# An mLSTM layer with two feed-forward blocks: the 64-by-64 products of each attention tile in one group, a 128-row spreading product, fixed PSUM banks, and a last store over three queues

## The chip, the cores and the metric

The kernel runs on one core of a Trainium2 chip, in one launch. The metric is the device time of one execution in microseconds (us), lower is better. TensorE (PE) multiplies, VectorE (DVE), ScalarE (ACT) and GpSimd (POOL) work on elements, SyncE (SP) issues most transfers.

## What is computed

An mLSTM recurrence over 768 positions, for 2 batches of 8 heads of width 40, whose output (1536 tokens of 320) passes two feed-forward blocks of inner width 2048:

```python
for t in range(S):
    m_new = np.maximum(f_gate[:, :, t] + m, i_gate[:, :, t])
    f_stab = np.exp(f_gate[:, :, t] + m - m_new)
    i_stab = np.exp(i_gate[:, :, t] - m_new)
    m = m_new
    C = f_stab * C + i_stab * outer(v_t, k_t)
    n = f_stab * n + i_stab * k_t
    y[:, :, t] = sigmoid(o_gate_t) * (C @ q_t) / np.maximum(abs(n @ q_t), 1.0)
x = hinge2(x @ w_in) @ w_out
x = softplus(x @ w_in2) @ w_out2
```

## The kernel before

**Attention.** The recurrence is done by chunks: 12 tiles of 64 positions, both batches side by side on the 128 partitions (64 each). For tile n, TensorE makes: `bc` (L422), one product that spreads the forget gates of all heads over the partitions, with 64 rows of weights (`sel`); `qkp` (L452), keys times queries, 16 products of 64 by 64; `pv` (L474), the masked weights times the values, and `pv` again (L482), the state times the decayed queries, 16 products each; `stp` (L521), the state's update, 16 products; and `tr` (L540), three 128-by-128 transposes of the result `y` into `xh`, the feed-forward input. Between them DVE makes the decay mask `f` by a scan over `bc` (L436) and multiplies it by `qkp` (L463), prepares `qd` (L467), the denominators `den` (L495, L496), `y` (L505), and adds `stp` to `state` (L534), which POOL has decayed before (L525). POOL also makes `vi`, `ve`, `m` and the gated `sig`. The small products use one half of the array's rows (64 or 40) and half of its columns; the profile counts each as two records, so 16 are shown as x32.

**Feed-forward.** Tokens go in three blocks of 512. A step is one slice of 128 of the inner width: `h`, 8 products of 128x512 (L620, `up`), an activation on ACT and DVE, a split of the result into a high part `gh` and a low part `gl` (L669, L673), and the products of `down1` (8 of 128x512, L687 to L693) or `down2` (12 of 128x320, L750 to L752), which accumulate over 16 steps. There are 48 steps in each of the two feed-forward blocks. Each weight slice is loaded once (`raw`, L565, 704 KB), unpacked from 64-bit floats by two ACT operations and one DVE operation (`v`, L571 to L582), and split into high and low parts `w` (L593 on ACT, L600 on DVE or POOL). Two `raw` and two `v` buffers exist. The slices of the first feed-forward block are needed in the first 16 steps, which is also where tiles 4 to 7 run.

**The order.** A planner (class `Plan`) takes every operation with an estimated cost and, for some PE operations, a place `at`, works out due times, and emits each engine's instructions in the order of a list schedule; the order is fixed when the program is built. Feed-forward step g has place 10·g. The list `where` gives each tile its places: tiles 0 to 3 (`n < EARLY`) come before the first step, in what is called the head below; of tiles 4 to 11 each four run within 16 steps. While PE has nothing else at the start, the planner inserts `fill` products (L387), which change no result.

**PSUM.** Eight banks: `h` has two, `d0`, `d1`, `d2` one each, and the pool `a` three, which `bc`, `qkp`, `pv`, `stp` and `tr` take in rotation.

**The end.** The last block's four output tiles `o` are copied from PSUM (L765 on DVE, L767 on ACT) and each is stored by two transfers (L782), one from SP's queue and one from ACT's.

Of the kernel before, what the change touches and what calls it, by code (L numbers as in the profile page):

```python
# [30 lines left out]
WARM = 200  # L31
EARLY = 4


class Plan:
# [15 lines left out]

    def add(self, eng, cost, emit, reads=(), writes=(), new=(), at=None, after=0.0, port=False, duty=1.0, fill=False):
        self.tasks.append(dict(
            eng=eng, cost=cost, emit=emit, reads=list(reads), writes=list(writes),
            new=list(new), at=at, after=after, port=port, duty=duty, fill=fill, i=len(self.tasks)))

# [14 lines left out]
    def run(self, start):  # L71
# [57 lines left out]
        for i in range(n):  # L129
            if not left[i]:  # L130
                enter(i)
        port, filling = 0.0, True
# [46 lines left out]
def mlstm_moe_moe(ctx: ExitStack, tc: tile.TileContext, gates, qk, tok, ident, w1, w2, out):  # L179
    nc = tc.nc  # L180

    def pool(name, bufs, stack=ctx, **kw):
        return stack.enter_context(tc.tile_pool(name=name, bufs=bufs, **kw))

    BUFS = dict(raw=2, v=2, w=NF, u=3, gh=4, gl=3, xr=1, qk=2, tok=2, m=1, f=2, dec=2, qd=2, sig=2, vi=2, ve=2,
                den=2, y=2, v2=10, e=3, o=4, h=2, d0=1, d1=1, d2=1, a=3)
    pools, tiles = {}, {}
# [3 lines left out]
    for name in ("raw", "v", "w", "u", "gh", "gl", "xr"):  # L191
        pools[name] = pool(name, BUFS[name])
    for name in ("h", "d0", "d1", "d2", "a"):
        pools[name] = pool("ps_" + name, BUFS[name], space=PSUM)
# [97 lines left out]
    for s, (c0, c1) in enumerate(SEG):  # L292
# [68 lines left out]
        def t(s=s, c0=c0, c1=c1):  # L361
            ps = new("a", ("isp", s), [128, 4, 16])
            for k in range((c1 - c0) // 2):
                nc.tensor.transpose(ps[:, k, :], tiles["gi",][:, (c0 + 2 * k) * C:(c0 + 2 * k + 2) * C], id_sb[0:16, 0:16])
        add("pe", 0.02 * (c1 - c0), t, duty=0.5, reads=[(gi, s), (("id",),)], writes=[(("isp", s),)],
            new=[("a", ("isp", s))], at=-100 + s)

# [23 lines left out]
    def attention(c, at):  # L391
# [17 lines left out]

        qtag, btag = ("d0", "h") if n < EARLY else ("a", "a")  # L410

        def t(e):
            eng = nc.gpsimd if e == "pool" else nc.vector
            eng.tensor_tensor(
                out=new("m", ("m", n), [64, H, C], F32R), in0=gr[:, None, c * C:(c + 1) * C].to_broadcast([64, H, C]),
                in1=own[:, :, None].to_broadcast([64, H, C]), op=ALU.mult)
# [36 lines left out]
        add("pe", 1.1, t, duty=0.75, reads=[(QK,)], writes=[(("qkp", n),)], new=[(qtag, ("qkp", n))], at=at[0])  # L453

# [22 lines left out]
        add("pe", 1.1, t, duty=0.75, reads=[(FK,), (VI,)], writes=[(("pv", n),)], new=[("a", ("pv", n))], at=at[1])  # L477
        if c > 0:
            def t():
                for h in range(H):  # L480
                    for p, k in zip(half, keys):
                        nc.tensor.matmul(  # L482
                            tiles["pv", n][p, h, :], tiles[QD][k, h, :], state[k, h, :], start=False, stop=(h == H - 1))
            add("pe", 1.0, t, duty=0.75, reads=[(QD,), (ST,)], writes=[(("pv", n),)], at=at[1] + 0.5)

# [4 lines left out]
        def t():  # L490
            nc.scalar.activation(out=new("den", DN, [128, H, 1]), in_=tiles["pv", n][:, :, D:V1], func=ACTF.Abs)
        add("act", 0.16, t, reads=[*ATT, (("pv", n),)], writes=[(DN,)], new=[("den", DN)])

# [20 lines left out]
        if c < NC - 1:  # L514
            def t():
                ps = new("a", ("stp", n), [128, H, V1])
# [5 lines left out]
            add("pe", 1.1 if n < EARLY else 0.75, t, duty=0.75, reads=[(TK,), (VE,)], writes=[(("stp", n),)], new=[("a", ("stp", n))], at=at[1] + 1)  # L522
            if c > 0:
# [13 lines left out]
        def t():  # L537
            ps = new("a", ("tr", n), [128, 3, L])
            for i in range(3):
                nc.tensor.transpose(ps[:, i, :], tiles[Y][:, i * 128:(i + 1) * 128], id_sb)  # L540
        add("pe", 0.34, t, reads=[(Y, 0), (Y, 1)], writes=[(("tr", n),)], new=[("a", ("tr", n))], at=at[2])
        j, o = block_of(n * L)
# [17 lines left out]
    def weights(l, f):  # L560
# [11 lines left out]
        add("act", act(WC), t, reads=[(R,)] + ([*ATT] if l else []), writes=[(V,)], new=[(tag, V)])  # L572
# [5 lines left out]
        add("act", act(WC), t, writes=[(V,)])  # L578

# [8 lines left out]
    def weights_split(l, f, V):  # L588
        W = ("w", l, f)

        def t():
            w = new("w", W, [128, 2 * WC], F32R)
            nc.scalar.copy(w[:, 0:WC], tiles[V].bitcast(F32))  # L593
        add("act", act(WC), t, reads=[(V,)], writes=[(W, 0)], new=[("w", W)])

# [137 lines left out]
    def down2(j, f, at):  # L733
# [21 lines left out]
        if e:  # L755
            for i in range(m):
# [13 lines left out]

                if j == len(BLOCKS) - 1 and i == m - 1:
                    copies([("act", 0, DM // 2), ("dve", DM // 2, DM)])
                else:
                    copies([("dve" if i % 2 else "act", 0, DM)])

                for b in range(B):
                    q = "act" if j == len(BLOCKS) - 1 and b else "sp"

                    def t(b=b, i=i, O=O, q=q):
                        r0 = b * S + (t0 // L + i) * C  # L780
                        eng = nc.scalar if q == "act" else nc.sync
                        eng.dma_start(out=out[r0:r0 + C, :], in_=tiles[O][64 * b:64 * b + 64, :])  # L782
                    add(q, 0.6, t, reads=[(O, 0), (O, DM // 2)], after=2.0)
# [106 lines left out]
```

## Time and profile before

| | |
|---|---|
| three timed runs | 437.7, 437.94, 439.21 us (median 437.94) |
| the profiled execution, its own time | 440.93 us |
| its span in the trace | 439.1 us |
| PE busy | 427.7 us (97% of the span) |
| DVE, ACT, POOL busy | 296.2, 272.7, 52.9 us |
| granted TensorE clock, mean | 0.993 of full speed |
| read from HBM, written | 38.57 MB, 2.02 MB |

The time around the span is 440.93 − 439.1 = 1.83 us. Busy time of PE is modelled: matmuls are pipelined, so that a 128x512 product of 0.39 us is followed by the next one after 0.23 us. What PE spends is therefore read from one start to the next.

### The profile page before, as it was taken

The numbers are of one execution on the slowest core, as the hardware profiler recorded it, in microseconds if no ns is written. First come the engines' busy times: TensorE is split into PE (matmuls) and PEld (weight loads), VectorE is DVE, ScalarE is ACT, GpSimd is POOL, SyncE is SP. The second block draws the span as 40 slices with busy tenths as digits, with TensorE's granted clock in tenths as the row PEclk, the third lists the DMA queues.
The fourth block names the chain that finished last, engine by engine and source line by source line (L and its number), as shares of the span: only waits on it lengthen the run. The fifth ranks groups of instructions, "written<-read, shape, count | busy, mean of one in ns | idle before, by whom it ended". The sixth has DMA issues, their size and how long they took to land.

```text
span 439.1 us, 8150 instructions
## 1 busy us (share of the span) xinstructions
PE 427.7 (97%) x3315; PEld 354.9 (81%) x3315; DVE 296.2 (67%) x467; ACT 272.7 (62%) x474; POOL 52.9 (12%) x64
## 2 busy tenths in 40 slices
PE   8989999998999999999999999999999999999994
PEld 3766887877787878787888888899999999999994
DVE  6989999978548454556877779555565555655552
ACT  4645988786426445478999987555555555555551
POOL 3743241312122211000000000000000000000000
PEclk9999999998999999999999999999999999999998
DMA  6889657657031200034354500000020000010002
GB/s 231 260 300 301 214 183 234 214 194 233 18 120 37 84 1 1 1 117 156 110 187 157 170 29 0 0 2 0 1 52 9 1 1 0 24 37 2 0 1 60
DMA packets 12214, 41.11 MB, mean 94 GB/s; under 512 B 1905, under 2 KB 3569, under 8 KB 12177
## 3 DMA queue, kind: packets, MB, share of 16 engines
q1 hardware_dynamic: 11856, 40.27, 28.1%
q8 instruction: 26, 0.43, 0.4%
q10 hardware_dynamic: 320, 0.33, 0.3%
q14 instruction: 12, 0.09, 0.1%
HBM read 38.57 MB, written 2.02 MB: 92 GB/s over the span
## 4 chain that ended last, share of the span: by engine, by line
PE 87%; DMA 4%; DVE 3%; ACT 3%; issue 2%; POOL 0%; SPq 0%; DVEq 0%; POOLq 0%; ACTq 0%
PE h L620 39%; PE d L692 5%; PE d L691 5%; PE d L693 4%; PE d L751 3%; PE a L751 3%; PE a L752 3%; PE d L752 3%; PE d L750 3%; PE a L750 3%; PE d L687 3%; PE pv L474 2%; PE d L688 2%; PE pv L482 2%; DMA qk<-in_qk_dram 2%
## 5 line engine op out<-in xcount | busy, mean ns | idle before, releaser
L620 PE MATMUL h<-xh,w 128*128 128x512 f32 x576 | 180.3, 395 | 1.1 <-ACT xh L545 0.6
L620 PEld LDWEIGHTS h<-xh,w 128*128 128x128 f32 x576 | 108.0, 188 | 25.2 <-DVE u L637 1.1
L673 DVE TENSOR_TENSOR gl<-u,gh 128x512 fp32r<-128x512 f32 x96 | 69.0, 720 | 41.7 <-ACT gh L669 36.5
L669 ACT CAST gh<-u 128x512 fp32r<-128x512 f32 x96 | 59.5, 620 | 52.2 <-DVE u L660 32.9
L620 PE MATMUL h<-xl,w 128*128 128x512 f32 x192 | 75.7, 394 | 0.1
L660 DVE TENSOR_TENSOR u<-u,e 128x512 f32<-128x512 f32 x48 | 33.2, 692 | 31.8 <-ACT e L656 31.8
L656 ACT ACTIVATE e<-e 128x512 f32<-128x512 f32 x48 | 30.4, 633 | 34.6 <-DVE e L651 34.5
L637 DVE SCALAR_TENSOR_TENSOR u<-u,h 128x512 f32<-128x512 f32 x48 | 32.7, 681 | 15.7 <-ACT u L633 15.2
L628 ACT ACTIVATE u<-h 128x512 f32<-128x512 f32 x48 | 28.4, 592 | 22.3 <-PE h L620 22.0
L620 PEld LDWEIGHTS h<-xl,w 128*128 128x128 f32 x192 | 36.0, 188 | 6.8 <-DVE xl L550 0.4
L692 PE MATMUL d<-gh,w 128*128 128x512 f32 x96 | 37.9, 394 | 0.0
L691 PE MATMUL d<-gh,w 128*128 128x512 f32 x96 | 37.8, 394 | 0.0
L693 PE MATMUL d<-gl,w 128*128 128x512 f32 x96 | 37.6, 391 | 0.0
L651 DVE SCALAR_TENSOR_TENSOR e<-u,h 128x512 f32<-128x512 f32 x48 | 33.0, 687 | 6.0
L582 DVE SCALAR_TENSOR_TENSOR v<-raw,v 128x704 int32<-128x704 int32 x32 | 29.5, 925 | 9.7 <-ACT v L575 9.7
L647 ACT ACTIVATE u<-h 128x512 f32<-128x512 f32 x48 | 28.7, 599 | 10.2 <-PE h L620 10.2
L600 DVE TENSOR_TENSOR w<-v,w 128x704 fp32r<-128x704 f32 (+2 forms) x46 | 29.7, 673 | 4.2 <-ACT w L593 4.1
L571 ACT ACTIVATE v<-raw 128x704 f32<-128x704 int8 x32 | 27.0, 842 | 8.2 <-DMA raw<-in_w_dram 5.7
L633 ACT ACTIVATE u<-u 128x512 f32<-128x512 f32 x48 | 30.2, 630 | 0.4
L751 PE MATMUL d<-w,gh 128*128 128x320 f32 x96 | 29.6, 309 | 0.0
L752 PE MATMUL a<-w,gl 128*128 128x320 f32 x96 | 29.6, 309 | 0.0
L752 PE MATMUL d<-w,gl 128*128 128x320 f32 x96 | 29.6, 309 | 0.0
(92 smaller groups left out, 672.4 us busy)
## 6 DMA issues: line engine op xcount, KB each, us to landing
raw<-in_w_dram SPq DMA_DIRECT2D x32, 704.0 KB, 4.2
qk<-in_qk_dram SPq DMA_DIRECT2D x12, 512.0 KB, 5.0
tok<-in_tok_dram SPq DMA_DIRECT2D x12, 496.0 KB, 4.8
dec<-scr_d SPq DMA_DIRECT2D x22, 128.0 KB, 4.4
out_dram<-o SPq DMA_DIRECT2D x20, 80.0 KB, 2.1
out_dram<-o ACTq DMA_DIRECT2D x4, 80.0 KB, 2.2
consts<-in_ident_dram SPq DMA_DIRECT2D x1, 132.0 KB, 2.6
gf<-in_gates_dram SPq DMA_DIRECT2D x1, 48.0 KB, 2.0
```

The costliest lines, as they stand in the source:

```text
L620: nc.tensor.matmul(hp, a, x, start=(i == 0), stop=(i == len(ops) - 1))
L637: nc.vector.scalar_tensor_tensor(out=tiles[U], in0=tiles[U], scalar=1.0, in1=tiles[HP], op0=ALU.min, op1=ALU.max)
L651: nc.vector.scalar_tensor_tensor(out=new("e", E, [128, n]), in0=tiles[M], scalar=-2.0, in1=tiles[HP], op0=ALU.mult, op1=ALU.add)
L656: nc.scalar.activation(out=tiles[E], in_=tiles[E], func=ACTF.Softplus)
L660: nc.vector.tensor_tensor(out=tiles[M], in0=tiles[M], in1=tiles[E], op=ALU.add)
L669: nc.scalar.copy(new("gh", GH, [128, n], F32R), tiles[G])
L673: nc.vector.tensor_tensor(out=new("gl", GL, [128, n], F32R), in0=tiles[G], in1=tiles[GH].bitcast(F32), op=ALU.subtract)
L691: nc.tensor.matmul(d[i], hi[:, k], gh, start=s, stop=False)
L692: nc.tensor.matmul(d[i], lo[:, k], gh, start=False, stop=False)
L693: nc.tensor.matmul(d[i], hi[:, k], gl, start=False, stop=e)
L751: nc.tensor.matmul(d, gh[:, k], lo, start=False, stop=False)
L752: nc.tensor.matmul(d, gl[:, k], hi, start=False, stop=e)
```

## The change

1. **Places.** `GROUP` gives each of the tiles 4 to 11 one place, every 34 units from 23 on. `pv`, the state product and `stp` of a tile stand there, and `qkp` of the next tile right behind them (`where[n - 1][2] + 1.5`). `bc` stands 25 units ahead of its group, `tr` 15 behind.
2. **The planner** knows which products are small (`small=True`): once it has emitted a small one it prefers others that are due within 8 units (`STAY`), and it adds 0.1 to a product's cost at a change of kind (`SWITCH`). In the first 60 units DVE, ACT and POOL may wait for a more urgent operation (`PATIENT`). `act(c)` is estimated somewhat higher.
3. **The spreading product** has 128 rows in place of 64: `sel`, `own`, `m` and `gr` are 128 rows high (rows beyond the gates are zero).
4. **PSUM.** The pool `a` becomes three pools of one bank. From tile 4 on `bc` and `stp` use `ax`, `qkp` uses `ay`, `pv` and `tr` use `az`; ahead of that `qkp` alternates between `d0` and `d1`.
5. **Operations.** In the second feed-forward block the cast of `w` may run on DVE too. `den` and the unpacking of the weights depend on the table load, so that it cannot come between them.
6. **The last block's stores** go over SP (four), POOL (two, output tiles 0 and 1) and ACT (two, tiles 2 and 3), and the last tile is copied whole by DVE.

```diff
+GROUP = [23 + 34 * i for i in range(8)]
...
+    PATIENT, MARGIN, SHARE, UNTIL = ("dve", "act", "pool"), 3.0, 0.4, 60.0
+    SWITCH, STAY = 0.1, 8.0
...
                 i = min(near, key=lambda i: (due[i], i))
+                if e == "pe" and small:
+                    i = min((k for k in near if ts[k]["small"] and due[k] < due[i] + self.STAY), key=lambda k: due[k], default=i)
+                if e in self.PATIENT and now < self.UNTIL:
+                    urgent = [k for k in q if due[k] < due[i] - self.MARGIN and now < begin[k] < now + ts[i]["cost"] * self.SHARE]
+                    if urgent:
+                        i = min(urgent, key=lambda k: (begin[k], k))
...
-                    t["dur"] = self.clock(now, t["cost"], t["duty"])
+                    t["dur"] = self.clock(now, t["cost"] + (self.SWITCH if t["small"] != small else 0.0), t["duty"])
+                    small = t["small"]
...
-                den=2, y=2, v2=10, e=3, o=4, h=2, d0=1, d1=1, d2=1, a=3)
+                den=2, y=2, v2=10, e=3, o=4, h=2, d0=1, d1=1, d2=1, ax=1, ay=1, az=1)
...
-    id_sb, own, side = consts[:, 0:128], consts[0:64, 128:136], consts[0:64, 136:264]
+    id_sb, own, side = consts[:, 0:128], consts[:, 128:136], consts[:, 136:264]
...
-    sel = const.tile([64, 128], F32R)
-    gr = const.tile([64, S], F32)
+    sel = const.tile([128, 128], F32R)
+    gr = const.tile([128, S], F32)
...
-        qtag, btag = ("d0", "h") if n < EARLY else ("a", "a")
+        qtag, btag, rtag = (f"d{n % 2}", "h", "ay") if n < EARLY else ("ay", "ax", "az")
...
-            new=[(btag, ("bc", n))], at=at[0] - 1)
+            new=[(btag, ("bc", n))], at=at[0])
...
-            ps = new("a", ("pv", n), [128, H, V1])
+            ps = new("az", ("pv", n), [128, H, V1])
...
-        def t():
+        def t(e="act"):
...
+                nc.vector.tensor_copy(w, v)
-        add("act", act(WC), t, reads=[(V,)], writes=[(W, 0)], new=[("w", W)])
+        add("act|dve" if l else "act", act(WC), t, reads=[(V,)], writes=[(W, 0)], new=[("w", W)])
...
-                if j == len(BLOCKS) - 1 and i == m - 1:
-                    copies([("act", 0, DM // 2), ("dve", DM // 2, DM)])
-                else:
-                    copies([("dve" if i % 2 else "act", 0, DM)])
-
+                copies([("dve" if i % 2 else "act", 0, DM)])
                 for b in range(B):
-                    q = "act" if j == len(BLOCKS) - 1 and b else "sp"
+
+                    q = ("sp", "pool", "sp", "pool", "sp", "act", "sp", "act")[B * i + b] if j == len(BLOCKS) - 1 else "sp"
...
-    where, g0 = {}, 0
...
-                where[first + i] = [10 * (g0 + (4 * i + k) * 4 / m) + 3 for k in (0, 1, 3)]
...
+    where = {n: [-61 + 10 * n, -60 + 10 * n, -57 + 10 * n, -54 + 10 * n] for n in range(EARLY)}
+    for n in range(EARLY, NC):
+        p = GROUP[n - EARLY]
+        where[n] = [p - 25, where[n - 1][2] + 1.5, p, p + 15]
```

On PE, around tiles 8 and 9 (the first number in a name is the tile; of `h` and `d` the last is the step), before:

```order
L620 MATMUL h_0_1_0_1662<-xh1_137,w_0_0_550 128x512 x3
L422 MATMUL bc_8_1675<-m_8_1473,sel_132 128x512
L452 MATMUL qkp_8_1679<-qk_8_1239 64x64 x16
L687 MATMUL d2_0_0_916<-gh_0_0_13_1590,w_0_13_1404 128x512
...
L620 MATMUL h_0_1_1_1717<-xh1_137,w_0_1_572 128x512 x3
L474 MATMUL pv_8_1728<-vi_8_1385,f_8_1696 64x41 x16
L482 MATMUL pv_8_1728<-state_135,qd_8_1420 64x41 x16
L521 MATMUL stp_8_1765<-ve_8_1712,tok_8_1348 40x41 x16
L687 MATMUL d2_0_0_916<-gh_0_0_14_1639,w_0_14_1477 128x512
```

and now:

```order
L486 MATMUL pv_8_1689<-vi_8_1428,f_8_1621 64x41 x16
L494 MATMUL pv_8_1689<-state_141,qd_8_1468 64x41 x16
L533 MATMUL stp_8_1726<-ve_8_1631,tok_8_1361 40x41 x16
L464 MATMUL qkp_9_1748<-qk_9_1386 64x64 x16
L635 MATMUL h_0_1_0_1770<-xh1_143,w_0_0_556 128x512
...
L708 MATMUL d1_0_0_917<-gl_0_0_13_1660,w_0_13_1466 128x512
L434 MATMUL bc_9_1802<-m_9_1623,sel_138 128x512
L635 MATMUL h_0_1_1_1805<-xh1_143,w_0_1_659 128x512
```

`bc` and `qkp` stood as a pair of their own one step ahead of the group; now `qkp` of tile 9 closes the group of tile 8, and `bc` of tile 9 stands alone among the 128-row products.

On PE, in the head, from `qkp` of tile 3 to the first `h`, before (the rows left out are 9, 2 and 11 fills):

```order
L452 MATMUL qkp_3_508<-qk_3_432 64x64 x16
L474 MATMUL pv_2_533<-vi_2_408,f_2_382 64x41 x16
L482 MATMUL pv_2_533<-state_135,qd_2_430 64x41 x16
L540 MATMUL tr_1_574<-consts_129,y_1_505 128x128 x3
...
L521 MATMUL stp_3_601<-ve_3_531,tok_3_405 64x41 x16
...
L474 MATMUL pv_3_631<-vi_3_476,f_3_482 64x41 x16
L482 MATMUL pv_3_631<-state_135,qd_3_578 64x41 x16
L540 MATMUL tr_2_676<-consts_129,y_2_623 128x128 x3
...
L452 MATMUL qkp_4_711<-qk_4_464 64x64 x16
L422 MATMUL bc_4_736<-m_4_629,sel_132 128x512
L540 MATMUL tr_3_740<-consts_129,y_3_728 128x128 x3
```

and now (left out are 1, 2, 7 and 7 fills):

```order
L464 MATMUL qkp_3_534<-qk_3_446 64x64 x16
L533 MATMUL stp_2_561<-ve_2_456,tok_2_347 64x41 x16
L552 MATMUL tr_1_581<-consts_135,y_1_482 128x128 x3
...
L486 MATMUL pv_3_594<-vi_3_486,f_3_464 64x41 x16
L494 MATMUL pv_3_594<-state_141,qd_3_579 64x41 x16
L533 MATMUL stp_3_640<-ve_3_515,tok_3_426 64x41 x16
L552 MATMUL tr_2_665<-consts_135,y_2_587 128x128 x3
...
L434 MATMUL bc_4_676<-m_4_638,sel_138 128x512
...
L552 MATMUL tr_3_698<-consts_135,y_3_688 128x128 x3
...
L464 MATMUL qkp_4_719<-qk_4_470 64x64 x16
L533 MATMUL stp_4_742<-ve_4_715,tok_4_585 40x41 x16
```

`pv` of tile 2 now comes ahead of `qkp` of tile 3, `stp` of tile 4 has come in from behind the first two steps, and 17 fills stand where 22 stood.

At the end, on ACT before:

```order
L767 COPY o_2_0_4594<-d2_1_2_0_4152 128x320
L767 COPY o_2_2_4598<-a_1_2_2_4160 128x320
L767 COPY o_2_3_4600<-a_1_2_3_4164 128x160
L782 DMA out_0_dram<-o_2_0_4594 64x320
L782 DMA out_0_dram<-o_2_1_4596 64x320
L782 DMA out_0_dram<-o_2_2_4598 64x320
L782 DMA out_0_dram<-o_2_3_4600 64x320
```

and now, on ACT and then on POOL:

```order
L782 COPY o_2_0_4593<-d2_1_2_0_4151 128x320
L782 COPY o_2_2_4597<-ay_1_2_2_4159 128x320
L794 DMA out_0_dram<-o_2_2_4597 64x320
L794 DMA out_0_dram<-o_2_3_4599 64x320
...
L794 DMA out_0_dram<-o_2_0_4593 64x320
L794 DMA out_0_dram<-o_2_1_4595 64x320
```

ACT issues two transfers in place of four and copies no half tile; POOL issues the other two; SP's four stay.

## Rows read from the trace of the kernel before

**Rows 1.** Busy time by stretch: stretch, its length; PE, PEld, DVE, ACT, POOL busy (instructions); granted clock; DMA share; GB/s.

```profile
50.00:75.00 25.00, 25.00 (x223) 20.11 (x222) 23.87 (x39) 20.80 (x38) 8.35 (x10) 1.00 0.62 207
75.00:100.00 25.00, 24.48 (x243) 19.24 (x242) 21.96 (x37) 19.62 (x36) 5.68 (x6) 1.00 0.58 198
100.00:125.00 25.00, 23.83 (x217) 19.03 (x215) 16.47 (x28) 12.31 (x23) 5.00 (x6) 0.93 0.41 132
```

**Rows 2.** Chain that ended last, two steps of the second feed-forward stretch: start, length, what.

```profile
225.15 1.86 PE h L620 x8
228.85 1.86 PE h L620 x8
```

**Rows 3.** The same chain, 137 to 148 us, around tile 9.

```profile
139.05 0.42 PE bc L422
139.47 1.08 PE qkp L452 x32
140.55 0.43 PE d L687
...
144.46 1.06 PE pv L474 x32
145.52 0.93 PE pv L482 x32
146.46 0.61 PE stp L521 x32
```

**Rows 4.** Instructions of PE in the head, in order of time: start, length, instruction, [idle before].

```profile
27.50 1.15 PE L452 MATMUL qkp<-qk 64*64 64x64 f32 x32 [1.20 <-DMA qk<-in_qk_dram]
28.45 1.11 PE L474 MATMUL pv<-vi,f 64*64 64x41 f32 x32
...
35.40 1.11 PE L482 MATMUL pv<-state,qd 40*64 40x41 f32 x32
...
36.82 2.54 PE L387 MATMUL fill<-warm 128*128 128x512 bf16 x11
...
40.80 0.55 PE L540 MATMUL tr<-consts,y 128*128 128x128 f32 x3
41.91 0.50 PE L620 MATMUL h<-xh,w 128*128 128x512 f32 x1 [0.57 <-ACT xh L545]
```

**Rows 5.** PE at tile 7, in order of time.

```profile
103.55 1.13 PE L474 MATMUL pv<-vi,f 64*64 64x41 f32 x32 [1.17 <-DVE f L463]
```

**Rows 6.** DVE ahead of that, in order of time.

```profile
101.85 0.95 DVE L600 TENSOR_TENSOR w<-v,w 128x64 fp32r<-128x64 f32 x2
102.72 0.68 DVE L463 TENSOR_TENSOR f<-qkp,f 128x512 f32<-128x512 f32 x1
```

**Rows 7.** Busy time by stretch, as in Rows 1: small products in the head, and tile 7.

```profile
14.40:20.20 5.80, 5.66 (x162) 5.08 (x161) 5.70 (x10) 3.18 (x7) 4.43 (x5) 1.00 0.78 222
...
104.40:109.00 4.60, 4.60 (x80) 4.09 (x77) 4.12 (x10) 2.19 (x5) 1.74 (x2) 0.63 0.76 234
```

**Rows 8.** Line L782, the stores: duration ns min/median/max, first and last start us.

```profile
L782 SPq DMA_DIRECT2D out_dram<-o x20: 467/567/603, 323.7 to 434.5; - x20
...
L782 ACTq DMA_DIRECT2D out_dram<-o x4: 557/612/784, 433.9 to 436.0; - x4
...
DMA to landing us min/median/max: 2.0/2.1/2.3
```

**Rows 9.** Copies at the end, in order of time.

```profile
432.62 0.49 DVE L765 COPY o<-a 128x320 f32<-128x320 f32 x1 [2.00 <-PE a L752]
...
433.50 0.33 DVE L765 COPY o<-a 128x160 f32<-128x160 f32 x1 [0.39 <-PE a L752]
```

**Rows 10.** Tile 5: PE, then DVE, in order of time.

```profile
64.10 0.79 PE L521 MATMUL stp<-ve,tok 64*40 64x41 f32 x32
...
68.71 1.00 DVE L534 TENSOR_TENSOR state<-stp,state 40x328 f32<-40x328 f32 x2
```

**Rows 11.** Chain that ended last, the one weight load on it.

```profile
83.06 7.27 DMA raw<-in_w_dram
```

More of the change, by code (lines that the diff above doesn't have):

```diff
@@ L50, in __init__, with add @@
         self.fast, self.busy, self.edge = False, 0.0, self.WINDOW
-    def add(self, eng, cost, emit, reads=(), writes=(), new=(), at=None, after=0.0, port=False, duty=1.0, fill=False):
+    def add(self, eng, cost, emit, reads=(), writes=(), new=(), at=None, after=0.0, port=False, duty=1.0, fill=False, small=False):
         self.tasks.append(dict(
             eng=eng, cost=cost, emit=emit, reads=list(reads), writes=list(writes),
-            new=list(new), at=at, after=after, port=port, duty=duty, fill=fill, i=len(self.tasks)))
+            new=list(new), at=at, after=after, port=port, duty=duty, fill=fill, small=small, i=len(self.tasks)))
     def clock(self, now, cost, duty):
@@ L131, in run @@
                 enter(i)
-        port, filling = 0.0, True
+        port, filling, small = 0.0, True, False
         for _ in range(n):
@@ L192, in mlstm_moe_moe @@
         pools[name] = pool(name, BUFS[name])
-    for name in ("h", "d0", "d1", "d2", "a"):
+    for name in ("h", "d0", "d1", "d2", "ax", "ay", "az"):
         pools[name] = pool("ps_" + name, BUFS[name], space=PSUM)
@@ L361, in t @@
         def t(s=s, c0=c0, c1=c1):
-            ps = new("a", ("isp", s), [128, 4, 16])
+            ps = new("ax", ("isp", s), [128, 4, 16])
             for k in range((c1 - c0) // 2):
@@ L414, in t @@
             eng.tensor_tensor(
-                out=new("m", ("m", n), [64, H, C], F32R), in0=gr[:, None, c * C:(c + 1) * C].to_broadcast([64, H, C]),
-                in1=own[:, :, None].to_broadcast([64, H, C]), op=ALU.mult)
+                out=new("m", ("m", n), [128, H, C], F32R), in0=gr[:, None, c * C:(c + 1) * C].to_broadcast([128, H, C]),
+                in1=own[:, :, None].to_broadcast([128, H, C]), op=ALU.mult)
         add("dve|pool", vec(512), t, port=True, reads=[*ATT, (("gr",), s, 0), (("gr",), s, 1), (("id",),)], writes=[(("m", n),)],
@@ L452, in t @@
                     nc.tensor.matmul(ps[p, h, :], q()[p, 1, h, :], q()[p, 0, h, :], start=True, stop=True)
-        add("pe", 1.1, t, duty=0.75, reads=[(QK,)], writes=[(("qkp", n),)], new=[(qtag, ("qkp", n))], at=at[0])
+        add("pe", 1.1, t, duty=0.75, small=True, reads=[(QK,)], writes=[(("qkp", n),)], new=[(qtag, ("qkp", n))], at=at[1])
         if c < NC - 1:
@@ L476, in t @@
                         start=(h == 0), stop=(c == 0 and h == H - 1))
-        add("pe", 1.1, t, duty=0.75, reads=[(FK,), (VI,)], writes=[(("pv", n),)], new=[("a", ("pv", n))], at=at[1])
+        add("pe", 1.1, t, duty=0.75, small=True, reads=[(FK,), (VI,)], writes=[(("pv", n),)], new=[("az", ("pv", n))], at=at[2])
         if c > 0:
@@ L483, in t @@
                             tiles["pv", n][p, h, :], tiles[QD][k, h, :], state[k, h, :], start=False, stop=(h == H - 1))
-            add("pe", 1.0, t, duty=0.75, reads=[(QD,), (ST,)], writes=[(("pv", n),)], at=at[1] + 0.5)
+            add("pe", 1.0, t, duty=0.75, small=True, reads=[(QD,), (ST,)], writes=[(("pv", n),)], at=at[2] + 0.5)
         def t():
@@ L491, in t @@
             nc.scalar.activation(out=new("den", DN, [128, H, 1]), in_=tiles["pv", n][:, :, D:V1], func=ACTF.Abs)
-        add("act", 0.16, t, reads=[*ATT, (("pv", n),)], writes=[(DN,)], new=[("den", DN)])
+        add("act", 0.16, t, reads=[*ATT, *TAB, (("pv", n),)], writes=[(DN,)], new=[("den", DN)])
         def t():
@@ L515, in t @@
             def t():
-                ps = new("a", ("stp", n), [128, H, V1])
+                ps = new("ax", ("stp", n), [128, H, V1])
                 for h in range(H):
@@ L521, in t @@
                         nc.tensor.matmul(ps[o, h, :], tk()[p, k0:k0 + w], tiles[VE][p, h, :], start=True, stop=True)
-            add("pe", 1.1 if n < EARLY else 0.75, t, duty=0.75, reads=[(TK,), (VE,)], writes=[(("stp", n),)], new=[("a", ("stp", n))], at=at[1] + 1)
+            add("pe", 1.1 if n < EARLY else 0.75, t, duty=0.75, small=True, reads=[(TK,), (VE,)], writes=[(("stp", n),)], new=[("ax", ("stp", n))], at=at[2] + 1)
             if c > 0:
@@ L537, in t @@
         def t():
-            ps = new("a", ("tr", n), [128, 3, L])
+            ps = new(rtag, ("tr", n), [128, 3, L])
             for i in range(3):
                 nc.tensor.transpose(ps[:, i, :], tiles[Y][:, i * 128:(i + 1) * 128], id_sb)
-        add("pe", 0.34, t, reads=[(Y, 0), (Y, 1)], writes=[(("tr", n),)], new=[("a", ("tr", n))], at=at[2])
+        add("pe", 0.34, t, reads=[(Y, 0), (Y, 1)], writes=[(("tr", n),)], new=[(rtag, ("tr", n))], at=at[3])
         j, o = block_of(n * L)
@@ L571, in t @@
             nc.scalar.activation(out=v.bitcast(F32), in_=top, func=ACTF.Prelu, bias=-56.0, alpha=2.0 ** -40)
-        add("act", act(WC), t, reads=[(R,)] + ([*ATT] if l else []), writes=[(V,)], new=[(tag, V)])
+        add("act", act(WC), t, reads=[(R,), *TAB] + ([*ATT] if l else []), writes=[(V,)], new=[(tag, V)])
         def t():
@@ L577, in t @@
                 alpha=2.0 ** 40)
-        add("act", act(WC), t, writes=[(V,)])
+        add("act", act(WC), t, reads=TAB, writes=[(V,)])
         def t():
@@ L589, in weights_split @@
         W = ("w", l, f)
-        def t():
-            w = new("w", W, [128, 2 * WC], F32R)
-            nc.scalar.copy(w[:, 0:WC], tiles[V].bitcast(F32))
-        add("act", act(WC), t, reads=[(V,)], writes=[(W, 0)], new=[("w", W)])
+        def t(e="act"):
+            w, v = new("w", W, [128, 2 * WC], F32R)[:, 0:WC], tiles[V].bitcast(F32)
+            if e == "act":
+                nc.scalar.copy(w, v)
+            else:
+                nc.vector.tensor_copy(w, v)
+        add("act|dve" if l else "act", act(WC), t, reads=[(V,)], writes=[(W, 0)], new=[("w", W)])
         def t(e):
```

18 lines of the change are left out of this document (5 added, 13 removed).

## The prediction

> **What bounds the kernel now.** I read the busy time by stretch first. From 50 us on PE is busy nearly all the time, at full clock but for one stretch [rows 1]; the page's 97% in the table says the same. The chain that ended last then shows what PE does there: one step of the first feed-forward block takes 3.70 us from `h` to `h`, of which the 8 products of `h` take 1.86, 0.23 each [rows 2]. So time is won where PE spends more than that per product, or waits. There are four such places. At every attention tile the small products and `bc` cost more than their columns [rows 3]. In the head PE has fills and waits until the first `h` at 41.91 [rows 4]. At tile 7 PE waits 1.17 us for the mask [rows 5], and the clock falls right behind it [rows 7]. At the end eight stores go out one behind the other on two queues [rows 8]. Against that, DVE is busy 23.87 and 21.96 of 25 us between 50 and 100 us, ACT 20.80 and 19.62 [rows 1]: in the 16 steps that unpack the first weights, PE has an engine close behind it.
>
> **Fewer changes of form, tiles 5 to 11.** In the chain around tile 9, `bc` takes 0.42, `qkp` 1.08, and the first 128-row product behind them 0.43 in place of 0.23; `pv`, the state product and `stp` take 1.06, 0.93 and 0.61, and then a 128-row product pays 0.20 again [rows 3]. Beyond the plain steps a tile so costs 0.42 + 1.08 + 0.20 = 1.70 for the pair and 1.06 + 0.93 + 0.61 + 0.20 = 2.80 for the group. Now `qkp` stands in the group. What it costs among small products is seen in the head, where it runs straight into `pv`: 28.45 − 27.50 = 0.95 [rows 4]. No row shows a `bc` of 128 rows among 128-row products; the nearest is a product of `h`, which has the same 512 columns and the same width of weights, 0.23 [rows 2]. The other end is the 0.42 that it takes with 64 rows. I take 0.23, because such a product then differs in nothing that the rows show from its neighbours. The pair thus costs 0.95 + 0.23 = 1.18 in place of 1.70: 0.52 a tile, seven tiles, **−3.6 us** (−2.3 if `bc` stays at 0.42). The Trainium skill's page "TensorE: Matmul & The Clock Gate" (section "Why this matters for your kernels") speaks against that step: a single product with few rows takes as long as one with 128, so the wider `bc` would by itself gain nothing. By that rule alone the sum is −2.3, by the row of `h` −3.6; the 0.19 between them is what I ascribe to the change of form, not to the rows.
>
> **The head.** All that lies between `qkp` of tile 3 and the first `h` is PE work in a fixed order, so I add up the new order from the same point, the landing of the keys of tile 3 (27.50) [rows 4]. Small groups count 0.95 each (the state product 0.93), a `tr` 0.4 (my reading of 0.55 less the overlap), a fill 2.54/11 = 0.23 [rows 4]: `qkp` 0.95, `stp` 0.95, `tr` 0.4, one fill 0.23, `pv` 0.95, state product 0.93, `stp` 0.95 and 0.1 for the change, `tr` 0.4, two fills 0.46, `bc` 0.23, seven fills 1.61, `tr` 0.4, seven fills 1.61, `qkp` 0.95, `stp` 0.61 and two changes 0.4. That is 12.1, so the first `h` would start at 39.6, 2.3 ahead of 41.91. The 0.57 us that PE waits there for `xh` is part of that, since 3.0 us of other work now stand between `tr` and `h`. `stp` of tile 4 (0.61 and a change) is done by then, which it was not before: another 0.7. The last `tr` might be late: it came 40.80 − 35.40 = 5.4 us behind the start of tile 3's state product [rows 4], and in the new order it stands 0.93 + 1.05 + 0.4 + 0.46 + 0.23 + 1.61 = 4.7 behind it, so up to 0.7 may be lost. I take **−2.8** (0 to −3.0: nothing, if the elements of y or the weights are what comes last; 3.0 if the `tr` is in time).
>
> **The wait at tile 7.** PE waited 1.17 us for DVE [rows 5], whose product with the mask stood behind two subtractions for a weight slice [rows 6]. Behind that wait the granted clock was 0.63 over 4.6 us [rows 7], which is 4.6 × 0.37 = 1.7 us lost. In the new order `bc` and `qkp` stand about two and a half steps (9 us) ahead of `pv` in place of one, so this particular wait goes: **−2.9**. What hides DVE's work is then that distance. If DVE is as late as before elsewhere, 0.
>
> **New waits in the 16 steps of the first weights.** PE would now come to a given step 2.8 us earlier, and by tile 7 another 1.5; the weights must come as much earlier. DVE has 1.13 and 3.04 us idle in the two 25 us stretches [rows 1], so it cannot deliver all of that. Five tiles instead of four stand in these steps, which puts the mask work of one more tile on DVE (its product alone 0.68), while the low parts of two slices move to POOL and one comes back, −0.95 [rows 6]. A weight load took as long as 7.27 us on the chain [rows 11], with only two `raw` buffers, each freed by DVE. Between no loss and the whole gain of this stretch (2.8 + 2.9 + 1.5 = 7.2) I take a third, **+2.5**.
>
> **The end.** ACT's four stores start from 433.9 to 436.0 and the last of them ends the kernel; SP's last starts at 434.5 [rows 8]. With two stores ACT is done soon after the last copy. That copy is now a whole tile on DVE, 0.49 in place of 0.33 [rows 9], ends at 433.99, and no ACT half follows. SP's four stay as they are, so 434.5 is the new last start: **−1.5**. No transfer was issued by POOL in the trace. Its two belong to the first two tiles, ready at about 432.6 and 433.1, and 2.3 us to landing [rows 8] would have to become 4.2 before they end later than SP's; with POOL at ACT's worst issue time (0.784) they are well ahead. Bounds: 0 to −1.5. The Trainium skill's page "DMA: Bandwidth & Descriptors" (specifications) gives the only price, a first byte after about 1 us on this path against 0.6; my estimate from it is that each POOL store lands 0.4 later, and the sum stays −1.5.
>
> **Costed at nothing.** The cast on DVE in the second block, the dropped table loads and the later `tr` lie beside a PE that never waits there; the ready weights are the cover. The banks cost nothing as long as they are free in time (below).
>
> **Sum** on the profiled execution: −3.6 − 2.8 − 2.9 + 2.5 − 1.5 = −8.3, 440.93 to 432.6. The median of the runs is 2.99 lower than that execution. If the clock fall at tile 7 is not in those runs, the gain on them is 5.4 and the time 432.5; if it is, 437.94 − 8.3 = 429.6. I take **431**.
>
> **The rivals.** *The weights eat it.* PE arrives earlier at step 4 and waits there for `w`, as DVE's load allows. The gain of 7.2 in these steps is lost; what stays are tiles 8 to 11 (4 × 0.52 = 2.1) and the end (1.5): 437.94 − 3.6 = 434.3. DVE at 95% and 88% [rows 1] speaks for it, the 4.2 us that DVE still sat idle there, and the slice it loses to POOL, against it.
>
> *One bank per product.* `bc` of the next tile shares `ax` with `stp` and can only start once DVE has added `stp` to the state. For tile 5 that addition began 68.71 − 64.10 = 4.6 us after `stp` and took 1.0 [rows 10]; the next `bc` now follows `stp` after its own 0.61, `qkp` 0.95, a change 0.2 and one step's `h` or `down1` 1.86, 3.6 us. PE would wait 2.0 us at tiles 5, 6 and 7, 6 us in all less what DVE gains by it: 435 to 437, no faster than the bound of a measurement. Against it: DVE's queue at that place is another one now.
>
> *The clock falls in every group, and it is slower.* A group is now 128 small products (3.8 us) in place of 96 and a pair. The one time that the clock fell was while such a group ran, behind a wait of 1.17 us [rows 5, 7]. If the group alone does it, each costs 1.7, eight of them 13.6, and the time is 431 + 13.6 = 444.6; from five groups on there is no gain left. Against it, the head ran small products from 14.40 to 20.20 at 1.00 [rows 7]: that is longer than a group. What differs is only the idle time ahead of it.
>
> *Nothing waits.* Without the +2.5, and with all four terms in full: 437.94 − 10.8 = 427.1, and some 426 if a few small waits of the first steps go too.
>
> **How the numbers follow.** Forecast 429 to 433: 0.45. Nothing waits, 425.5 to 429: 0.20. Weights, 433 to 435.7: 0.17. Banks or deeper waits, 435.7 to 440.1: 0.12. Clock, above 440.1: 0.06. The range 425.5 to 435.7 holds the first three, 0.82. A measurement tells about 0.5% (2.2 us) from no change, so faster means under 435.75: 0.82; within: 0.12; slower: 0.06.
>
> **What would show it.** Right: no 64-row `bc`, its successor 0.23 later; one 0.43 product per tile, behind `qkp`; a tile's extra on PE in the third block near 2.80 + 1.18 and `tr`; the first `h` near 39.6; full clock from 100 to 125 us; the last store starting near 434.5 less the gain. Wrong: PE waiting for `w` or for `u` between steps 4 and 15, a PE wait at `bc` released by DVE's `state`, a clock below 1.00 behind a group, or a POOL store that lands last.

## The result and the profile after

The changed kernel took **431.15 us** (median of four runs, 429.86 to 432.5) against 437.82 for the kernel before (437.55 to 439.21) on the same chip: a ratio of 0.9842, 95% interval 0.9805 to 0.9878, so 1.6% faster, clear of no change. One of the later runs of the kernel before took 2289.43 us and is left out of the ratios below. The profiled execution of the changed kernel took 431.06, with a span of 429.3; the one of before has 440.93 and 439.1. Three points divide the two spans, the start of the first and of the last group of `h` (first and last start in the rows of `h`) and the end:

| | first `h` | first to last `h` | last `h` to end | span |
|---|---|---|---|---|
| before | 41.91 | 384.1 | 13.1 | 439.1 |
| after | 41.05 | 375.95 | 12.3 | 429.3 |
| difference | -0.9 | -8.1 | -0.8 | -9.8 |

So most of the gain lies between the first and the last `h`, called the body below; what comes ahead of it is the head, what comes behind it the end. The busy time by stretch (columns as in [rows 1]) shows it: in the three stretches from 50 us on PE is busy all of the time, at full clock, where before it missed 0.52 and 1.17 us and the clock was 0.93 in the third. The first three rows are the head: a wait, and a low clock behind it.

```profile
14.00:16.00 2.00, 0.76 (x28) 0.65 (x24) 2.00 (x3) 1.98 (x5) 0.01 (x1) 1.00 0.75 160
16.00:18.00 2.00, 2.00 (x52) 2.00 (x50) 1.94 (x3) 0.96 (x3) 1.12 (x1) 0.62 0.76 280
18.00:20.00 2.00, 2.00 (x46) 2.00 (x42) 1.95 (x5) 0.00 (x0) 1.16 (x2) 0.53 0.78 262
...
50.00:75.00 25.00, 25.00 (x224) 20.57 (x223) 24.67 (x45) 23.21 (x42) 9.87 (x9) 1.00 0.63 215
75.00:100.00 25.00, 25.00 (x334) 21.00 (x333) 22.96 (x44) 21.05 (x37) 6.97 (x7) 1.00 0.70 239
100.00:125.00 25.00, 25.00 (x224) 20.68 (x223) 17.09 (x29) 11.51 (x23) 6.79 (x8) 1.00 0.42 131
```

The chain that ended last shows a tile's group and the next `bc`, where [rows 3] stood before: `qkp` takes 0.95 in the group, `bc` 0.23, and the `h` behind `bc` its plain 1.86. Only the `h` behind the group pays 0.20.

```profile
111.86 1.06 PE pv L486 x32
112.92 0.93 PE pv L494 x32
113.85 0.62 PE stp L533 x32
114.47 0.95 PE qkp L464 x32
115.42 2.06 PE h L635 x8
...
119.32 0.23 PE bc L434
119.55 1.86 PE h L635 x8
```

PE in the head, in order of time ([rows 4] before). Two waits stand there, for DVE's masked product of tile 0 and for `y` of tile 2, which has to read bank `az` before `pv` of tile 3 may write it.

```profile
15.72 1.34 PE L486 MATMUL pv<-vi,f 64*64 64x41 f32 x32 [1.24 <-DVE f L475]
...
28.10 1.16 PE L464 MATMUL qkp<-qk 64*64 64x64 f32 x32
...
31.35 1.13 PE L486 MATMUL pv<-vi,f 64*64 64x41 f32 x32 [0.71 <-DVE y L517]
...
40.34 0.78 PE L533 MATMUL stp<-ve,tok 64*40 64x41 f32 x32
41.05 0.50 PE L635 MATMUL h<-xh,w 128*128 128x512 f32 x1
```

The stores of the last block ([rows 8] before): the last one starts at 425.5, 8.5 behind the last `h` (before 10.0), but one takes 3.0 to land (before 2.3 at most).

```profile
L794 SPq DMA_DIRECT2D out_dram<-o x4: 466/544/553, 423.6 to 425.5; - x4
...
L794 POOL DMA_DIRECT2D out_dram<-o x2: 529/618/707, 424.2 to 425.0; - x2
L794 ACTq DMA_DIRECT2D out_dram<-o x2: 556/578/600, 424.5 to 425.1; - x2
...
DMA to landing us min/median/max: 2.0/2.4/3.0
```

The store of 3.0 is SP's from 424.8 and lands at 427.9, ahead of the last one. The last store to start also lands last. By itself, first in the changed kernel and then in the kernel before:

```profile
L794 SPq DMA_DIRECT2D out_dram<-o x1: 553/553/553, 425.5 to 425.5; - x1
...
DMA to landing us min/median/max: 2.7/2.7/2.7
...
L782 ACTq DMA_DIRECT2D out_dram<-o x1: 607/607/607, 436.0 to 436.0; - x1
...
DMA to landing us min/median/max: 2.1/2.1/2.1
```

### The profile page after: what moved, and what is told of

Read it like the earlier page. It is cut to its first block, busy times and chain, and to the rows that moved or that the text cites. A ratio compares the mean times of both kernels' runs of the same rounds, so it can differ in the third digit from the quotient of the medians.

```text
span 429.3 us, 8134 instructions
## 1 busy us (share of the span) xinstructions
PE 420.4 (98%) x3303; PEld 354.6 (83%) x3308; DVE 297.4 (69%) x473; ACT 266.6 (62%) x463; POOL 59.6 (14%) x68
## 4 chain that ended last, share of the span: by engine, by line
PE 94%; DVE 3%; issue 1%; ACT 1%; DMA 0%; POOL 0%; POOLq 0%; SPq 0%; DVEq 0%
PE h L635 42%; PE d L707 5%; PE d L706 5%; PE d L708 5%; PE d L766 3%; PE d L767 3%; PE d L765 3%; PE pv L486 3%; PE d L702 3%; PE d L703 3%; PE pv L494 2%; PE qkp L464 2%; PE stp L533 2%; PE fill L399 1%; PE ay L766 1%; PE az L767 1%
## 5 line engine op out<-in xcount | busy, mean ns | idle before, releaser
L688 DVE TENSOR_TENSOR gl<-u,gh 128x512 fp32r<-128x512 f32 x96 | 66.3, 691 | 39.8 <-ACT gh L684 37.4
L643 ACT ACTIVATE u<-h 128x512 f32<-128x512 f32 x48 | 28.6, 596 | 13.5 <-PE h L635 13.1
L662 ACT ACTIVATE u<-h 128x512 f32<-128x512 f32 x48 | 28.8, 601 | 12.6 <-PE h L635 12.3
L766 PE MATMUL d<-w,gh 128*128 128x320 f32 x96 | 29.6, 309 | 0.0
L765 PE MATMUL d<-w,gh 128*128 128x320 f32 x96 | 29.5, 307 | 0.0
L615 DVE TENSOR_TENSOR w<-v,w 128x704 fp32r<-128x704 f32 (+2 forms) x43 | 27.0, 658 | 3.2 <-ACT w L606 3.2
```

Source lines behind the costliest of these rows:

```text
L688: nc.vector.tensor_tensor(out=new("gl", GL, [128, n], F32R), in0=tiles[G], in1=tiles[GH].bitcast(F32), op=ALU.subtract)
L765: nc.tensor.matmul(d, gh[:, k], hi, start=s, stop=False)
L766: nc.tensor.matmul(d, gh[:, k], lo, start=False, stop=False)
```

## The experiments

Times of one chip differ from the next by 1 to 2 us (the kernel before had a median of 437.82 above and of 439.0 to 440.1 beside the runs below), so times are given as ratios to it, and the terms are read from the body, which repeats to 0.1 us in the changed kernel (375.95, 375.9, 375.9).

**Both kernels again, unchanged.**

> The kernel before, unchanged, for a second profile. My theory puts 2.9 us of the gain on a wait of PE at tile 7 (1.17 us) and the clock behind it (1.7 us), and splits the difference between the profiled execution (440.9) and the median (437.8) on whether they occur in every execution. If they are in every execution: again a wait of 1.0 to 1.3 at the state product or pv of tile 7 and a stretch at a clock near 0.6, span 436 to 439. If they are of one execution only: no stretch under 0.9 after 50 us, span about 436.

> The changed kernel, unchanged, for a second profile. In its first profile PE waited 1.24 us for the masked product of tile 0 at 14.5 us and ran at a clock of 0.53 to 0.62 from 16 to 20 us. If wait and clock belong to the order of the instructions, both are there again and the first h starts at 41.0 (within 0.3). If they are of one execution, the clock is 1.00 there and the first h starts up to 1.5 us earlier.

Before: 439.7, span 437.9. The waits of PE from 41 us on (time in all, times, longest) hold the wait at tile 7 again, 1.17 us at 103.70, and one of 0.9 at 94.99; the clock is 1.00 from 100 to 125 us.

```profile
PE pv L474 <- DVE f L463: 1.2, 1, 1.2
PE h L620 <- DVE u L637: 0.9, 1, 0.9
PE h L620 <- DVE xl L550: 0.6, 1, 0.6
```

So the wait at tile 7 came in both executions of this kernel, the fall of the clock in one. The changed kernel: 434.78, body 375.9, but the first `h` at 44.83. PE in the head, in order of time: the wait for `y` is 2.48, and the products behind it take 1.9 to 2.0 in place of 1.1; the granted clock is 0.54 from 33 to 40 us.

```profile
32.54 1.14 PE L486 MATMUL pv<-vi,f 64*64 64x41 f32 x32 [2.48 <-DVE y L517]
33.46 1.93 PE L494 MATMUL pv<-state,qd 40*64 40x41 f32 x32
35.12 1.98 PE L533 MATMUL stp<-ve,tok 64*64 64x41 f32 x32
...
44.83 0.50 PE L635 MATMUL h<-xh,w 128*128 128x512 f32 x1
```

**The two halves of the first term, one undone at a time.**

```diff
-    sel = const.tile([128, 128], F32R)
+    sel = const.tile([64, 128], F32R)
...
```

(and `own`, `side`, `gr` and `m` likewise)

> The changed kernel with the spreading product over 64 rows again (its operands are 64 rows high), everything else in the same order. My theory: the product behind it pays 0.19 more, 0.42 in place of 0.23, at seven tiles, +1.3 us, 432.5. Rival (a single product with few rows takes as long as a full one, and the form makes no difference): 0.23 for each, time the same within 0.3.

```diff
-        add("pe", 1.1, t, duty=0.75, small=True, reads=[(QK,)], ...
+        add("pe", 1.1, t, duty=0.75, small=n < EARLY, reads=[(QK,)], ...
...
-        where[n] = [p - 25, where[n - 1][2] + 1.5, p, p + 15]
+        where[n] = [p - 25, p - 24.5, p, p + 15]
```

> The changed kernel with qkp of tiles 4 to 11 out of the group of small products: it stands alone, behind bc, between 128-row products. My theory: each time a change of form into (0.13) and out of (0.20) it, 0.33 at seven tiles and once more for a stp that stands apart too, +2.3 to +2.6 us, 433.5. Rival (grouping gives nothing, the gain was the waits): within 0.5 of the changed kernel. Both together with the 64-row product would give back the 3.6 of the first term.

With 64 rows (ratio 0.987, 0.9829 to 0.9911; body 379.3) the chain shows more than either theory: `bc` itself takes 0.42, and the `h` behind it 2.06.

```profile
120.81 0.42 PE bc L434
121.23 2.06 PE h L635 x8
```

That is 0.19 and 0.20, 0.39 a tile, 2.7 for seven; of the other 0.6, 0.4 is a wait at one `tr`. With `qkp` apart (ratio 0.9848, 0.9809 to 0.9887; body 379.4), `qkp` takes 1.08 and its successor 0.19 more:

```profile
120.14 0.24 PE bc L434
120.37 1.08 PE qkp L464 x32
121.45 2.05 PE h L635 x8
```

Eight such changes at 0.33 (seven `qkp` and one `stp` that stands alone) and `stp` of tile 4, which moved into the body (0.71), make 3.35 of the 3.45. So a wide `bc` alone saves 0.19 a tile (0.23 + 1.08 + 0.20 against 1.70), grouping alone 0.13 (0.95 + 0.42 + 0.20), both together 0.52: as long as one 64-row product stands alone among the full ones, the change is still paid.

**Where the runs differ, and the banks.**

> The changed kernel, unchanged, timed beside the next three on one chip, with a third profile. From the first h to the last product it took the same within 0.1 in both profiles so far (375.9 from the first to the last h), while the first h itself began at 41.05 and 44.8. My theory: the body is again 375.9, PE does not wait after the first h, and the whole spread of the runs (about 430 to 435) is the head. Rival: the spread is in the body, which would then differ by 1 us or more.

Ratio 0.9831 (0.98 to 0.9861), body 375.9 without a wait, first `h` at 39.9, clock 1.00 throughout. In the three profiled executions of the changed kernel the body and the end (12.3) are the same, and all of the difference is the head.

```diff
-        qtag, btag, rtag = (f"d{n % 2}", "h", "ay") if n < EARLY else ("ay", "ax", "az")
+        qtag, btag, rtag = ("d0", "h", "ay") if n < EARLY else ("ay", "ax", "az")
+        ptag = "d1" if n in (1, 3) else "az"
...
-            ps = new("az", ("pv", n), [128, H, V1])
+            ps = new(ptag, ("pv", n), [128, H, V1])
```

> The changed kernel with a second PSUM bank for pv in the first four tiles (qkp gives up one of its two for it). In four profiles with the fixed banks PE waited 0.7, 2.5, 0.7 and 1.7 us at pv of tile 3 for DVE's product y of tile 2, which has to read the bank first. Theory (the fixed bank is what waits): that wait is gone and the first h comes 0.7 to 2 us earlier, at 39.5 to 40.5, the time 1 us lower. Rival (DVE is late in the head whatever the bank): PE waits at another product for DVE, first h at 41 or later, time the same within 0.5. The body stays at 375.9 by both.

Ratio 0.984 (0.9811 to 0.987). The wait for `y` was gone, but PE waited for DVE's `state` (0.6), `f` (0.5) and for keys (2.2), and the first `h` began at 42.8. The clock of this execution was 0.88 in its first 14 us, and the planner also moved other products of the head, so this supports the rival without proving it. The runs show only that a free bank brought no time (median 432.25, beside them 431.56).

**The fills.**

```diff
-            nc.tensor.matmul(tiles["fill",], warm[:, 0:128], warm, start=True, stop=True)
+            if i < 26:
+                nc.tensor.matmul(tiles["fill",], warm[:, 0:128], warm, start=True, stop=True)
```

> The changed kernel with only the first 26 of its 54 fill products; the last 28 (11 ahead of pv of tile 2 and 17 ahead of bc, tr and qkp) are left out, 6.4 us of PE time; they write nothing that is used. Theory (some of them stand in the way: 10 ran straight ahead of pv of tile 2 and put qkp of tile 3 at 28.10): first h 0.6 to 1.3 earlier, time 430 to 431 on the chip of the first result. Rival 1 (they fill waits only): PE waits more and the first h stays within 0.3. Rival 2 (without them the granted clock falls): a stretch at a clock near 0.5 to 0.6 between 24 and 41 us and the first h 1.5 to 3 later.

Ratio 0.9951 (0.992 to 0.9982), 5.9 us over the unchanged kernel's median beside it. By stretch (length; PE; clock; DMA share; GB/s):

```profile
25.00:30.00 5.00, 4.72 (x114) 0.69 0.65 188
...
35.00:40.00 5.00, 3.67 (x39) 0.50 0.92 315
```

Rival 2 holds, and by more than it said: where the fills had stood PE waited (2.39, 1.33 and 1.38 us), the clock fell, and the first `h` came at 44.7, against 39.9 beside it. All twelve runs had a lower mean clock (0.959 to 0.978) than any run of the unchanged kernel beside them (0.994 to 1.0). In the body `bc` waited 0.52 for DVE's `state`.

**The end.**

```diff
-  q = ("sp", "pool", "sp", "pool", "sp", "act", "sp", "act")[B * i + b]
+  q = ("sp", "act", "sp", "act", "sp", "act", "sp", "act")[B * i + b]
```

> The changed kernel with POOL's two stores of the last block issued by ACT instead, behind its copies, so that ACT issues four and SP four; all other orders are the same. ACT's last store then starts 1.2 us later, at 12.3 - 4.1 + 1.2 behind the last h, 0.8 behind SP's last. By the prediction's way (the end follows the last start): the end, counted from the last h, 12.3 to 13.1, +0.8. Rival (the end now hangs on one store that took 3.0 to land, and with four stores on ACT none did, as in the kernel before, 2.3): 12.7, +0.4 or less.

Ratio 0.9838 (0.9797 to 0.9879). ACT's last store starts 9.0 behind the last `h` (425.6 - 416.6), 0.5 later than the last one of after, and the end is at 12.2, no later than with POOL, since no store takes over 2.3:

```profile
L794 SPq DMA_DIRECT2D out_dram<-o x4: 467/559/723, 423.2 to 425.2; - x4
L794 ACTq DMA_DIRECT2D out_dram<-o x4: 552/564/599, 423.7 to 425.6; - x4
...
DMA to landing us min/median/max: 2.0/2.2/2.3
```

So the third queue gained nothing; by what is left of the edit, the 0.8 comes from the copy that is no longer cut in two. Before, ACT's four stores stood behind its half of the last tile, which waited for DVE's half (start, length, instruction, idle before):

```profile
433.86 0.29 ACT L767 COPY o<-a 128x160 f32<-128x160 f32 x1 [0.38 <-DVE o L765]
433.92 2.68 ACTq L782 DMA_DIRECT2D out_dram<-o  x4
```

The first of them started 7.9 behind the last `h`; here, without the half copy, it is 7.1.

One store for each tile, three from SP and one from ACT:

```diff
+                if j == len(BLOCKS) - 1:
+                    q = ("sp", "sp", "act", "sp")[i]
...
+                        eng.dma_start(out=out.rearrange("(b s) d -> b s d", b=B)[:, r0:r0 + C, :], in_=tiles[O])
```

> The changed kernel with one store of 128 rows per tile of the last block in place of two of 64: SP three, ACT one, POOL none. The last copy ends 4.6 us ahead of the end; the store can start right behind it, at 8.0 behind the last h in place of 8.5. If it lands like the small ones on SP (2.1): the end 11.4 to 11.7 behind the last h in place of 12.3, -0.7 us. If twice the bytes take longer to land (3.0 or more): 12.3, no gain. The time moves by less than a measurement can tell; the trace decides.

Ratio 1.0093 (1.0053 to 1.0133): slower than the kernel before. The body is 375.9, the end 23.5 behind the last `h`; what that was stands in the last section.

**What keeps PE from waiting in the body.**

```diff
-    where[n] = [p - 25, where[n - 1][2] + 1.5, p, p + 15]
+    where[n] = [p - 25, where[n - 1][2] + 1.5, p, p + 15] if n == EARLY else [p - 11, p - 10, p, p + 15]
```

(and `small` off for `qkp` of these tiles)

> The changed kernel with bc and qkp of tiles 5 to 11 one step ahead of pv, as in the kernel before, and so qkp alone again (bc keeps its 128 rows). In six profiles of kernels whose qkp stands about two and a half steps ahead of pv, PE waited in the body at most 0.4 us, against 1.7 and 2.7 in the two of the kernel before. Theory (the distance hides DVE's product with the mask): PE waits at pv of at least one of tiles 5 to 8 for DVE, 0.5 to 1.3 us; from first to last h 375.9 + 2.3 for qkp alone + the waits = 379 to 381 (382.5 with a clock fall behind one). Rival (the planner's other order of DVE's work hides it, whatever the distance): no such wait, 378.2.

Ratio 0.9858 (0.9811 to 0.9905), body 380.1. PE waited at `pv` of one tile for the product with the mask:

```profile
96.69 1.13 PE L486 MATMUL pv<-vi,f 64*64 64x41 f32 x32 [0.66 <-DVE f L475]
```

With 2.3 for `qkp` alone and waits of 0.25 and 0.18 elsewhere that makes 379.3; 0.8 is not accounted for.

```diff
-    PATIENT, MARGIN, SHARE, UNTIL = ("dve", "act", "pool"), 3.0, 0.4, 60.0
+    PATIENT, MARGIN, SHARE, UNTIL = ("dve", "act", "pool"), 3.0, 0.4, 0.0
...
-        add("act|dve" if l else "act", act(WC), t, reads=[(V,)], writes=[(W, 0)], ...
+        add("act", act(WC), t, reads=[(V,)], writes=[(W, 0)], ...
```

> The changed kernel without the planner's two new freedoms: no waiting for an urgent task in the first 60 us (UNTIL = 0), and the casts of the second block's weights on ACT alone. Theory (they gained nothing that a profile shows; the grouping did): PE does not wait after the first h, body 375.9 within 0.3, first h within 1 of 41. Rival (they are what took the waits away): waits of 0.5 or more in the body, 376.5 to 378.

Ratio 0.9889 (0.9842 to 0.9935), body 378.6; PE in the body, in order of time:

```profile
59.63 0.50 PE L635 MATMUL h<-xh,w 128*128 128x512 f32 x1 [0.61 <-DVE u L652]
...
74.32 0.50 PE L434 MATMUL bc<-m,sel 128*128 128x512 f32 x1 [0.74 <-DVE state L546]
```

My theory fell: without the two freedoms PE waits 1.5 us in the body (0.7 for `state`, 0.8 for `u`); the other 1.1, in part a `stp` that stands alone at 62.02, was not taken apart. No `pv` of the body waited. The head of this execution had the 1.2 wait at `pv` of tile 0 and then a clock of 0.50 from 18 to 30 us, and its first `h` began at 46.1.

**Fills in the place of the two waits.**

```diff
+            for _ in range({0: 5, 3: 3}.get(n, 0)):          # ahead of pv
+                nc.tensor.matmul(tiles["fill",], warm[:, 0:128], warm, start=True, stop=True)
```

> The changed kernel with 5 more fill products ahead of pv of tile 0 and 3 ahead of pv of tile 3 (1.15 and 0.69 us), where PE waited 1.0 to 1.2 and 0.5 to 2.5 us in most profiles of this order; nothing else moves. In four of them the granted clock fell to 0.5 to 0.6 behind one of these waits, for 3 to 14 us, and in those the first h began at 41.05, 43.2, 44.8 and 46.1, in the others near 40. Theory (the idle time in the head lets the clock fall, and that makes the runs differ): no wait of over 0.5 at pv of tile 0, clock 1.00 there, first h at 39.9 to 40.8 unless the wait for tile 3 is far over 0.7; runs within 429 to 432, ratio 0.978 to 0.982. Rival (the clock falls for another reason, or the fills stand in the way): first h at 41 or later, ratio 0.983 to 0.987.

Ratio 0.9847 (0.9809 to 0.9886), first `h` at 41.4. Both waits were gone, but a wait of 1.2 ahead of the first `bc` was followed by a clock of 0.50 from 13 to 16 us, and `bc` of a later tile waited 0.93 in the body. By the numbers the rival held: filling these two waits brought no time, so that they make the runs differ is not shown.

## Why the prediction was right, point by point

**What bounds the kernel**: right. PE is busy without a gap in the body, and time was won where it paid for a change of form or waited.

**Fewer changes of form, -3.6**: right. A tile costs 1.06 + 0.93 + 0.62 + 0.95 + 0.20 + 0.23 = 3.99 beyond `tr` and the plain steps, before 4.50 (2.80 + 1.70); seven tiles make 3.6. A check by the whole body agrees: without its waits and the 1.7 that I estimate for the clock, the body before is 380.7 in the first profile and 381.0 in the second, after 375.95. Of the 4.8 to 5.0 between them this term is 3.6 and the `stp` of tile 4 that moved to the head 0.9. The other end I gave, -2.3 for a `bc` that stays at 0.42, was too good: the product behind such a `bc` pays 0.20 too, and 0.13 × 7 = 0.9 would be left. By the Trainium skill's page "TensorE: Matmul & The Clock Gate" (section "Why this matters for your kernels") rows alone change nothing; the trace differs in that a 64-row product among 128-row ones costs 0.39 more, its own 0.19 and its successor's 0.20.

**The head, -2.8**: mis-sized, and its sign is shown only where the clock stays full. In the first pair of profiles the first `h` came 0.86 earlier with `stp` of tile 4 (0.7 and a change of 0.2) already done, so about -1.8. The step that failed is "All that lies between `qkp` of tile 3 and the first `h` is PE work in a fixed order, so I add up the new order from the same point, the landing of the keys". `qkp` no longer waited for that landing: it came at 28.10 behind `pv` and the state product of tile 2, 0.6 later, and PE waited 0.71 for `y`. The work itself was summed well: 41.05 - 28.10 - 0.71 = 12.24, against 12.1. In the other executions of this order that wait was 0.5 to 2.5, and the first `h` in all profiles of the changed kernel and its variants lay between 39.9 and 46.1, every one over 41 with a stretch below full clock ahead of it. At full clock throughout, the changed kernel began at 39.9, and at 40.7 without POOL's stores; the kernel before, at full clock in its head, at 41.1 and 41.9. With 41.05 and 44.83 in the other two executions of the changed kernel, that its head is shorter on the average is not shown.

**The wait at tile 7, -2.9**: right for the execution that I read. The wait of 1.17 is in both profiles of before, the clock's 1.7 in one. That the distance hides the mask product is supported by the kernel with `qkp` late, where such a wait came back with 0.66, and by the one without the two freedoms, which keeps the distance and had no wait at a `pv` in the body.

**New waits, +2.5**: wrong in sign. In six profiles of the body (the three of the changed kernel, the one with head banks, the one without POOL, the one with one store) PE never waited, and the 0.5 that it waited before for `u` went too. The step that failed is that DVE, with so little idle time, "cannot deliver all of that". It was busy 47.6 of the 50 us from 50 to 100 in place of 45.8, POOL 16.8 in place of 14.0, in an order that serves PE in time. The run without the two freedoms has 1.5 of waits in the body; which of the two removes them was not separated.

**The end, -1.5**: the last start moved by 1.5 as forecast (10.0 to 8.5 behind the last `h`), but the end only by 0.8, since the last store took 2.7 to land in place of 2.1. The step that failed is that the end follows the last start, with SP's stores landing as before.

**The sum**: -8.3 forecast, -9.8 between the two profiled spans: 3.6, 1.8, 2.9, 0.5 and 0.8, with 0.2 left over. That 431 was met to 0.15 is in part luck. The +2.5 was not lost and 0.5 came on top, while the head gave about 1.0 and the end 0.7 less. And the medians differ by only 6.7, since the profiled execution of before was 3.1 above its median; I had taken a value between the two readings without knowing which holds. The later runs of the kernel before lie between 436.3 and 443.9, so the profiled 440.93 was an ordinary one.

**The rivals.** *The weights eat it*: no wait for `w` in any body of the changed order. *One bank per product*: the mechanism exists, with 0.52, 0.74 and 0.93 at one `bc` in three of the experiments' bodies, not 2.0 at three tiles; in the head a bank is what `pv` of tile 3 waits for. *The clock falls in every group*: refuted, 1.00 in the body in all profiles of the changed kernel. The clock fell in the head, behind idle time, as the forecast had suspected, but not behind every such wait.

## What to carry to other kernels

A product of another form among full ones costs twice, at its own start and in the product behind it; price runs of equal form, not products, since two edits that gain 0.13 and 0.19 alone gained 0.52 together. When an engine near 95% looks like a limit, ask whether the order lets it serve the critical engine in time before charging the whole load. Split a span at fixed points: here the body repeats to 0.1 us, and all of the difference between three executions lies in a head of 40 to 45 us, where the clock fell behind some of the waits.

## What was not expected of the hardware

**The clock behind a wait.** A wait of 1.17 to 1.24 us ahead of small products was followed by full clock in some executions and by a stretch near 0.5 (1.2 GHz) in others of the same instructions: at tile 7 of the kernel before once in two profiles, at `pv` of tile 0 in the first profile of the changed kernel and in neither of the next two. Over all profiles such stretches lasted from 3 to some 13 us. What decides it stays open.

**A store over two engines.** The last of the four stores, one per tile, was started at 427.1, and the span ends at 442.6. By stretch (length; PE, PEld, DVE, ACT, POOL; clock; DMA share; GB/s) the DMA share is 0.13, as of two busy engines out of 16 (2/16 = 0.125), at 49 GB/s:

```profile
434.00:436.00 2.00, 0.00 (x0) 0.00 (x0) 0.00 (x0) 0.00 (x0) 0.00 (x0) 0.50 0.13 49
```

The Trainium skill's page "DMA: Bandwidth & Descriptors" (section "Why a DMA increments its semaphore by 16 and not by 1") has the rule: the number of engines must divide the slowest dimension of both sides, and the destination's was 2, the batches. The trace agrees; the stores of 64 rows before them landed in 2.1.

**POOL's stores and those beside them.** In the changed kernel POOL's two landed in 2.4 (median), ACT's in 2.6, and the slowest, SP's, in 3.0; the three profiles of it agree to 0.1. In the three profiles where POOL issued none, the two of before and the one without POOL's stores, none took over 2.3. The last of these differs from the changed kernel in the queue of two stores alone; why they slow the others is open.
